# Moving the first expert block's row fetch, turn and split into the last attention heads, and the quarter blocks' table to the fifth block

## The chip, the cores and the metric

The kernel runs on one core of a Trainium2 chip. The metric is the device time of one execution in microseconds (us). The engines named below are TensorE (PE; its weight loads are PEld), VectorE (DVE), ScalarE (ACT), GpSimd (POOL) and the queue of SyncE (SP), from which nearly all DMAs are issued.

## The reference

Attention over 8 batches and 8 heads, sequence 576, head width 64, with a causal mask and a bias from a running sum; its output is taken as 4608 tokens of width 512. Each token then goes to one of 8 experts (argmax of a gate) and through that expert's two matrices, and is scaled by the gate's probability. Cut to what matters:

```python
def _attn_ref(q, k, v, s):
    scores = scale * np.matmul(q, k.transpose(0, 1, 3, 2))
    cum = np.cumsum(np.maximum(s, 0.0), axis=-1)
    bias = -(cum[:, :, :, None] - cum[:, :, None, :])
    scores = np.where(causal, -1e9, scores + np.minimum(bias, 0.0))
    attn = softmax(scores)
    return np.matmul(attn, v)

def _moe_ref(x, modality_id, w_gate, modality_bias, w1, w2):
    logits = x @ w_gate + modality_bias[modality_id]
    e_idx, gate_w = argmax(logits), softmax(logits)[e_idx]
    for e in range(E):                       # E = 8, D = 512, F = 1024
        h = np.maximum(x[e_idx == e] @ w1[e], 0.0)
        out[e_idx == e] = gate_w * (h @ w2[e])
```

## The kernel before

**Attention.** The 64 (batch, head) pairs are worked two at a time: a "pair" index runs from 0 to 31, eight pairs for each of four groups of batches. Every pair has nine score tiles, so the loop in Attn.run has 288 steps k and a few more to run out. A step makes one score tile (PE, then DVE for mask and maximum, then ACT for the exponential), turns the tile of three steps earlier (trans) and goes on with a tail: probabilities times V (L474), a copy of the result (ACT, L477, and DVE, L481), a matmul that turns it to rows and adds the gate's logits (L492, L494, by way of the helper at L346), and a DVE multiplication that writes it to the tile x of its group (L497, L499). The second tail of the last pair is the last work of attention.

**Routing.** When a group of batches is done, Route.group computes the experts of its tokens, counts with a small matmul (L708), and scatters the rows by nine indirect DMAs from POOL (L732) to a list for each expert in DRAM. It is a generator; attention's loop runs a piece of it at each step (the list bg). Groups 0 to 2 are scattered (27 scatters) during attention, group 3 afterwards. From the counts of groups 0 to 2 Route.first makes a table t2 of six full blocks of 256 rows. Moe.early then reads expert and row of block 0 to registers and, from step 278 (EARLY), loads its first four weight chunks and splits them on POOL into a high and a low part (L963, L966).

**Experts.** All matrix products are made in three passes over high and low parts. A block of 256 rows takes eight weight chunks of 512 KB: four of w1 (matmuls at L1102) and four of w2 (L1077). Chunks are loaded by SP, copied (high part) by ACT (L965) and subtracted (low part) by DVE (L966); their buffers come in three sets, wca, wcb and wcc. The rows of a block are fetched by gather2: four DMAs for 512 columns (L1038) and one for the gate and token number (L1039). Moe.xt turns them on DVE into PSUM (L1052), and splits them by an ACT copy (L1054) and a DVE subtraction (L1055). This is done in the middle of the block before; for block 0 it is done at the start, after attention's pools have closed. ACT and DVE empty the two halves of a block's output (L1087, L1085), and POOL scatters it to the result (L1088).

**Order.** The program is ordered by a scheduler that takes, on each engine, the ready instruction of best priority; a with-block of high_priority moves its instructions forward by so many places, and issue_after puts instructions behind a given one on its engine, without a wait between engines. Block 0 is traced with an offset of 300 (PRI), group 3's routing with 900 (PRI2).

**Remaining tables.** Block 2 is preceded by Route.rest, some 65 small DVE instructions: the table t3 (12 full blocks) and then the table t4 of the quarter blocks (64 rows), which are worked at the very end. The call for each block is finish(k); in blocks 1 to 4 it also writes zero rows behind the lists (pad).

Of the kernel before, what the change touches and what calls it, by code (L numbers as in the profile page):

```python
# [7 lines left out]
F32 = mybir.dt.float32  # L8
F32R = mybir.dt.float32r
BF16 = mybir.dt.bfloat16  # L10
I32 = mybir.dt.int32
AF = mybir.ActivationFunctionType
ALU = mybir.AluOpType
# [4 lines left out]
P = 128  # L18
KW = 576
XW = 72  # L20
# [18 lines left out]
class Attn:  # L39
# [415 lines left out]
    def tail(self, st, g):  # L455

        nc = self.nc
        V, PT, x, h = st["V"], st["PT"], st["x"], st["h"]
# [4 lines left out]
        oT = self.oT  # L463
# [12 lines left out]
        self.wall = m.ins  # L476
        nc.scalar.copy(oT[:, q0:q0 + 256], o[:, :256])  # L477
        if g:
            for ab in range(2):
                r = slice(64 * ab, 64 * ab + 64)  # L480
                nc.vector.tensor_copy(oT[r, 512 + 64 * ab:576 + 64 * ab], o[r, 256:320])  # L481
        yield
# [13 lines left out]
        rv = rs[:, 4 * g:4 * g + 4].unsqueeze(2).broadcast_to([P, 4, XW])  # L496
        nc.vector.tensor_tensor(x[g][:, :, :, h], src.rearrange("p t (d r) -> p t d r", r=2), rv.rearrange("p t (d r) -> p t d r", r=2), ALU.mult)  # L497
        if g:
            nc.vector.tensor_scalar(x[2][:, 0, :, h], xo[:, 4 * XW:5 * XW].rearrange("p (d r) -> p d r", r=2), rs[:, 8:9], None, ALU.mult)  # L499

# [75 lines left out]
PRI = 300  # L576
PRI2 = 900
SCS = 5, 5, 4, 4
NRA, NRB = 2, 4
# [4 lines left out]
NGS = 0  # L584
EARLY = 278


class Route:
# [81 lines left out]
    def group(self, bp, x, psum, mm, then=None):  # L670
# [34 lines left out]

        of = ohb.rearrange("p t e -> p (t e)")
        for u in range(10):
            (mm or nc.tensor.matmul)(pp[:, 8 * u:80], self.tri[:, min(u, 1)], of[:, :80 - 8 * u], start=u == 0, stop=u == 9)  # L708
# [142 lines left out]
    def rest(self):  # L851
# [25 lines left out]
        nc.vector.scalar_tensor_tensor(base, ex, float(CAP), s, ALU.mult, ALU.add)  # L877
        self.t3 = self.rows("r", nb, 2, ex, base, cn)

        exh, bh, ch = ex[:, N3:], base[:, N3:], cn[:, N3:]  # L880
# [25 lines left out]
class Moe:  # L906
    def __init__(self, ctx, tc, R, w1, w2, ident, out):
        self.nc, self.tc, self.R, self.w1, self.w2, self.ident, self.out = tc.nc, tc, R, w1, w2, ident, out
        self.wa = ctx.enter_context(tc.tile_pool(name="mwa", bufs=1))
        self.wb = None  # L910
        self.n = 0
        self.last = [None] * 4
        self.hold = None
        self.late, self.stop = None, 1 << 30
        self.back = ()

    def open(self, ctx):
# [114 lines left out]
    def gather2(self, tb, b, r):  # L1032

        nc = self.nc
        xr = self.mx.tile([P, 8, P], F32, name="xr", bufs=2)
        tg = self.mx.tile([P, 2, 2], F32, name="tg", bufs=3)
        rows = self.R.lists[bass.ds(r, 2 * P), :]
        i = [nc.sync.dma_start(xr[32 * q:32 * q + 32], rows[:, P * q:P * q + P].rearrange("(t p) d -> p t d", p=32)).ins for q in range(4)]  # L1038
        i.append(nc.sync.dma_start(tg, rows[:, 512:514].rearrange("(u p) d -> p u d", u=2)).ins)  # L1039
        self.rows(tb, i)  # L1040
        oi = self.mp.tile([P, 2], I32, name="oi", bufs=3)
        nc.vector.tensor_tensor(oi, tg[:, :, 1], tb["past"][:, bass.ds(b, 1), :].rearrange("p b u -> p (b u)"), ALU.add)
        return (xr, tg), oi

# [212 lines left out]
    def early(self):  # L1257
# [5 lines left out]
        for j in range(self.NA):  # L1263
# [4 lines left out]
            yield False  # L1268

    def run(self, lst, early=False, then=None, routed=None):  # L1270

        def pre(k):
            tb, b, nu = getattr(self.R, lst[k][0]), lst[k][1], lst[k][2]
            if nu == 0:
                e, r = zip(*(self.regs(tb, b + q) for q in range(2)))
                self.stop = self.n + 14
            else:
                e, r = self.er if early and k == 0 else self.regs(tb, b)
            xg, oi = self.gather(tb, b, r, nu)
            x = self.xt(xg, nu) if k == 0 else None  # L1280
            W, self.more = self.weights(e, self.have if early and k == 0 else ()) if nu else self.weights2(e)
            for _ in range(0 if self.late is not None else 2 if k else 8):
                next(self.more, 0)
            return W, xg, oi, x
# [27 lines left out]
def build(tc, qkv, s, mid, wg, mb, w1, w2, out):  # L1312
    nc = tc.nc
    with ExitStack() as ctx:
# [9 lines left out]
        with ExitStack() as actx:  # L1324
# [18 lines left out]

            setup = {**A.more, 5: A.consts, 14: R.consts, 17: lambda: A.save(0), 26: lambda: A.save(1), 20: lambda: R.setup(mid, mb, A.t1p)}
            bg = A.run(32, newx, done, setup)
            assert len(bg) == 1
            for _ in range(NGS):
                next(bg[0][0])
        with ExitStack() as mctx:
# [3 lines left out]
            def routed():  # L1353
                with ExitStack() as after:
                    for i in M.tr:
                        after.enter_context(tc.issue_after(i.ins))
                    after.enter_context(tc.high_priority(offset=PRI2))
                    for _ in bg[0][0]:
                        pass
                xctx.close()  # L1360
                M.open2(mctx)

            def finish(k):
# [3 lines left out]
                if 1 <= k <= 4:  # L1367
                    with ExitStack() as after:
# [3 lines left out]
                        if k == 2:  # L1372
                            for _ in R.rest():
                                pass
# [35 lines left out]
```

## Time and profile before

| what | value |
|---|---|
| median of 3 runs | 818.26 us (817.53 to 819.53) |
| the profiled execution's own time | 818.24 us |
| its span, first to last instruction | 816.5 us |
| mean granted TensorE clock | 0.992 |
| PE busy | 796.9 us, 98% |
| DVE busy | 575.3 us, 70% |
| ACT busy | 529.7 us, 65% |
| POOL busy | 364.4 us, 45% |

Starts in the profile are in us from the first instruction. A timeline row gives start, length, engine, line, operation, output and inputs, shape and count, and in brackets how long the engine was idle before and what released it. Attention's last matmul ends at 376.3 us; the experts fill the rest. The granted clock is the share of full clock that TensorE was given; it is 1.00 in most windows.

### The profile page before, as it was taken

Reading aid. Unit: us, or ns where it says so; the run is one execution under the profiler, and the core shown is the slowest. Engines: PE = TensorE matmul, PEld = TensorE weight load, DVE = VectorE, ACT = ScalarE, POOL = GpSimd, SP = SyncE. Lnnn points to the kernel's source line nnn. Section 1 sums busy time; section 2 is a strip of 40 time slices with the busy share of each in tenths; the row PEclk is TensorE's granted clock in tenths of the full one; section 3 lists DMA queues with packets and bytes.
Section 4 is the critical chain, followed back from the end, with each engine's and each line's share of the span. In section 5 each row is a group of like instructions: output and inputs, shape, how many; then the busy total and the mean of one; then the engine's idle time right before and its main releaser. Section 6 shows DMA issues by size and latency. Waiting matters only on the chain. (4 is left out here: it accounts for less than half of the span.)

```text
span 816.5 us, 16747 instructions
## 1 busy us (share of the span) xinstructions
PE 796.9 (98%) x5548; PEld 681.4 (83%) x5548; DVE 575.3 (70%) x1441; ACT 529.7 (65%) x1196; POOL 364.4 (45%) x383
## 2 busy tenths in 40 slices
PE   7999999999999999998999799999999999999997
PEld 6777887888888888877888798889899989988884
DVE  7666667667666677767679677777877766777654
ACT  6888788888878888875463355555555554455553
POOL 8959778988699877993600111100000010000001
PEclk9999999999999999999999999999999999999999
DMA  7665556776557666738696968677887878786750
GB/s 237 178 197 184 181 184 198 228 240 191 173 183 224 200 184 183 238 130 277 205 366 235 313 224 270 223 248 241 266 259 225 263 253 268 243 269 222 249 194 29
DMA packets 88134, 181.17 MB, mean 222 GB/s; under 512 B 13753, under 2 KB 33081, under 8 KB 87918
## 3 DMA queue, kind: packets, MB, share of 16 engines
q1 hardware_dynamic: 82206, 160.03, 62.2%
q0 software_dynamic: 5840, 20.06, 6.3%
q8 instruction: 44, 0.72, 0.4%
q14 instruction: 44, 0.36, 0.1%
HBM read 143.59 MB, written 26.80 MB: 209 GB/s over the span
## 5 line engine op out<-in xcount | busy, mean ns | idle before, releaser
L1088 POOL DMA_INDIRECT out<-ys,oi x36 | 39.0, 1084 | 357.1 <-ACT ys L1087 264.8
L396 DVE CUSTOM_DVE_ANT_0 pe<-sp,mk 128x512 f32<-128x512 f32 (+3 forms) x256 | 122.4, 488 | 100.6 <-PE sp L394 90.5
L416 ACT ACTIVATE pe<-pe,mx 128x512 f32<-128x512 f32 (+3 forms) x256 | 144.9, 567 | 15.7 <-DVE mx L396 13.1
L433 PE MATMUL pt<-ident,pe 128*128 128x128 f32 x640 | 110.7, 278 | 0.8 <-ACT PT L437 0.5
L437 ACT COPY PT<-pt 128x512 f32<-128x512 f32 (+1 forms) x192 | 97.3, 510 | 20.1 <-PE pt L433 20.1
L372 PE MATMUL sp<-KA,QH 128*128 128x256 f32 (+2 forms) x256 | 102.4, 402 | 2.5 <-POOL KA L236 2.5
L1104 ACT ACTIVATE hT<-hp 128x512 fp32r<-128x512 f32 x72 | 43.2, 600 | 89.5 <-PE hp L1102 87.7
L474 PE MATMUL o<-PT,V 128*64 128x320 f32 (+4 forms) x896 | 100.7, 364 | 0.0
L474 PEld LDWEIGHTS o<-PT,V 128*64 128x64 f32 x896 | 58.6, 136 | 46.6 <-issue 14.5
L1102 PE MATMUL hp<-xT,wcb 128*128 128x256 f32 x648 | 90.6, 283 | 0.8 <-DVE hT L1105 0.6
L1102 PE MATMUL hp<-xT,wca 128*128 128x256 f32 x624 | 87.1, 284 | 2.6 <-ACT xT L1054 2.5
L326 POOL TENSOR_TENSOR KA<-rawk,KA 64x576 fp32r<-64x576 f32 x62 | 87.2, 1425 | 0.2
L433 PEld LDWEIGHTS pt<-ident,pe 128*128 128x128 f32 x640 | 75.9, 143 | 13.6 <-issue 5.3
L326 POOL TENSOR_TENSOR QL<-rawq,QH 64x576 fp32r<-64x576 f32 x62 | 86.7, 1413 | 0.2
L394 PE MATMUL sp<-KB,QL 76*128 76x256 f32 (+2 forms) x256 | 85.4, 337 | 0.0
L1102 PEld LDWEIGHTS hp<-xT,wcb 128*128 128x128 f32 x648 | 83.4, 188 | 1.9 <-DVE hT L1105 0.8
L1102 PEld LDWEIGHTS hp<-xT,wca 128*128 128x128 f32 x624 | 80.3, 193 | 3.6 <-issue 2.6
L1105 DVE SCALAR_TENSOR_TENSOR hT<-hp,hT 128x512 fp32r<-128x512 f32 x72 | 49.5, 688 | 47.2 <-ACT hT L1104 46.9
L1077 PE MATMUL y<-wcb,hT 128*128 128x512 f32 x336 | 80.7, 396 | 0.0
L1077 PEld LDWEIGHTS y<-wcb,hT 128*128 128x128 f32 x336 | 62.7, 188 | 14.6
L1102 PE MATMUL hp<-xT,wcc 128*128 128x256 f32 x456 | 65.3, 282 | 4.8 <-DVE xT L1055 2.9
L1102 PEld LDWEIGHTS hp<-xT,wcc 128*128 128x128 f32 x456 | 59.3, 191 | 6.3 <-DVE xT L1055 3.1
(284 smaller groups left out, 1603.1 us busy)
## 6 DMA issues: line engine op xcount, KB each, us to landing
wrbw<-in_w SPq DMA_DIRECT2D x104, 512.0 KB
wraw<-in_w SPq DMA_DIRECT2D x56, 512.0 KB
rawq<-in_qkv SPq DMA_DIRECT2D x31, 576.0 KB
rawk<-in_qkv SPq DMA_DIRECT2D x31, 576.0 KB
V<-in_qkv SPq DMA_DIRECT2D x32, 320.0 KB
xr<-lists SPq DMA_DIRECT2D x72, 128.0 KB
KB<-KA SPq DMA_DIRECT2D x62, 144.0 KB
lists<-z SPq DMA_DIRECT2D x8, 576.0 KB
```

Of the source, the lines that this page charges most:

```text
L326: self.last = nc.gpsimd.tensor_tensor(o, i, h, ALU.subtract).ins
L372: self.pe.append(self.nc.tensor.matmul(sp[:, :nn], QH[:, q0:q0 + P], self.KA[u][:, ab, :nn], start=True, stop=False).ins)
L394: self.pe.append(nc.tensor.matmul(sp[:, :nn], QL[:EXT, q0:q0 + P], KB[:EXT, ab, :nn], start=False, stop=True).ins)
L396: ins = nc.vector.tensor_tensor_reduce(out=t[:, :n], in0=sp[:, :n], in1=self.mk[:, 512 - n:512], scale=-0.125, scalar=3.0e38, op0=ALU.add, ...
L416: self.act = nc.scalar.activation(t[:, :n], t[:, :n], AF.Exp, bias=m, scale=-1.0, accum_out=st["sums"][:, o:o + 1]).ins
L433: self.pe.append(nc.tensor.transpose(out=pt[:, o:o + P], in_=pe[:, P * j:P * j + P], identity=self.ident).ins)
L437: cp(w[:, :, :, v:v + P], pt[:, :n * (1 + both)].rearrange("p (a j q) -> p a j q", a=1 + both, q=P))
L474: m = nc.tensor.matmul(o[r, f - q0:q1 - q0], V[:, ab, j, :], PT[:, ab, PTS * j + f if j < 4 else PTW - 64:PTS * j + q1 if j < 4 else PTW], ...
L1077: self.last[0] = nc.tensor.matmul(y[u], hT[:, a, f, P * u:P * u + P], W[4 + f // 2][:, c, 512 * (f % 2):512 * (f % 2) + 512], start=f == 0 ...
L1102: nc.tensor.matmul(hp[:, u], W[k][:, a, f:f + P], xT[:, c, k], start=k == 0 and i == 0, stop=k == 3 and i == 2)
L1104: hi = nc.scalar.activation(hs, hp, AF.Relu)
L1105: lo = nc.vector.scalar_tensor_tensor(hT[:, 1, 2 * m:2 * m + 2], hp, 0.0, hs.bitcast(F32), ALU.max, ALU.subtract)
```

## The change

- **Block 0's rows.** A new generator, Moe.early_rows, joins bg at step 275. When 27 scatters are issued and block 0's registers are known, it takes the two x tiles of group 2, which are scattered by then, as memory, and issues the five DMAs of the rows. It goes on at step 288 (TURN), after the last score tile: two DVE transposes, now from SBUF into SBUF, each followed by a copy on POOL (high part); at steps 289 and 290 one DVE subtraction each (low part), put behind the newest of the DVE steps called behind_x. Block 0 uses these tiles and no PSUM for them. The splits of w2's four chunks of block 0 are put behind attention's last ACT copy and last DVE multiplication (fin) instead of behind block 0's row split.
- **Group 3's routing.** The part up to the counting matmul keeps the offset 900; from that matmul on, with the scatters, it has 200 (PRI3).
- **Tables.** Route.rest stops after t3 in block 2; t4 is made when finish(4) is called.

```diff
@@ Attn.tail
-        nc.scalar.copy(oT[:, q0:q0 + 256], o[:, :256])
+        self.fin = [nc.scalar.copy(oT[:, q0:q0 + 256], o[:, :256])]
...
-                nc.vector.tensor_copy(oT[r, 512 + 64 * ab:576 + 64 * ab], o[r, 256:320])
+                self.behind_x = nc.vector.tensor_copy(oT[r, 512 + 64 * ab:576 + 64 * ab], o[r, 256:320])
...
-        nc.vector.tensor_tensor(x[g][:, :, :, h], ...)
+        self.fin.append(nc.vector.tensor_tensor(x[g][:, :, :, h], ...))
         if g:
-            nc.vector.tensor_scalar(x[2][:, 0, :, h], ...)
+            self.behind_x = nc.vector.tensor_scalar(x[2][:, 0, :, h], ...)
@@ Route.group
         of = ohb.rearrange("p t e -> p (t e)")
+        if not mm:
+            yield "mm"
@@ Route.rest
         self.t3 = self.rows("r", nb, 2, ex, base, cn)
+        yield "t3"
@@ Moe
+    def early_rows(self, pool, A):
+        nc, R = self.nc, self.R
+        while len(R.scat) < 27 or self.er is None:
+            yield False
+        a, b = (pool.tile([P, 4, XW // 2, 8, 2], F32, name="x").rearrange("p t d h r -> p (t d h r)") for _ in range(2))
+        tg, oi = R.c.tile([P, 2, 2], F32, name="tg0"), R.c.tile([P, 2], I32, name="oi0")
+        xr, xf = a[:, :1024].rearrange("p (t d) -> p t d", t=8), a[:, 1024:2048].rearrange("p (k n) -> p k n", k=4)
+        xT = b[:, :2048].bitcast(F32R).rearrange("p (a k n) -> p a k n", a=2, k=4)
+        self.fetch_rows(R.t2, self.er[1], xr, tg)
+        yield TURN
+        ks = [slice(0, 2), slice(2, 4)]
+        for k in ks:
+            A.hold[0] = nc.vector.transpose(out=xf[:, k].rearrange("p k (t n) -> p k t n", n=32),
+                                            in_=xr.rearrange("p t (d k) -> p k t d", k=4)[:, k]).ins
+            A.last = nc.gpsimd.tensor_scalar(xT[:, 0, k], xf[:, k], 1.0, 1.0, ALU.mult, ALU.mult).ins
+        for k in ks:
+            yield False
+            with self.tc.issue_after(A.behind_x.ins):
+                nc.vector.tensor_tensor(xT[:, 1, k], xf[:, k], xT[:, 0, k].bitcast(F32), ALU.subtract)
+        nc.vector.tensor_tensor(oi, tg[:, :, 1], R.t2["past"][:, 0], ALU.add)
+        self.first = ((None, tg), oi), xT
@@ Moe.run, pre(k)
-            xg, oi = self.gather(tb, b, r, nu)
-            x = self.xt(xg, nu) if k == 0 else None
+            if early and k == 0:
+                (xg, oi), x = self.first
+            else:
+                xg, oi = self.gather(tb, b, r, nu)
+                x = self.xt(xg, nu) if k == 0 else None
@@ build
+            setup[275] = lambda: M.early_rows(xps[0], A)
             bg = A.run(32, newx, done, setup)
+            M.tr = None, *A.fin
...
-                    for i in M.tr:
+                    for i in M.tr[1:]:
                         after.enter_context(tc.issue_after(i.ins))
-                    after.enter_context(tc.high_priority(offset=PRI2))
-                    for _ in bg[0][0]:
-                        pass
+                    with tc.high_priority(offset=PRI2):
+                        while next(bg[0][0]) != "mm":
+                            pass
+                    with tc.high_priority(offset=PRI3):
+                        for _ in bg[0][0]:
+                            pass
...
                         if k == 2:
-                            for _ in R.rest():
+                            rest.append(R.rest())
+                            while next(rest[0]) != "t3":
+                                pass
+                        if k == 4:
+                            for _ in rest[0]:
                                 pass
```

More of the change, by code (lines that the diff above doesn't have):

```diff
@@ L496, in tail @@
         rv = rs[:, 4 * g:4 * g + 4].unsqueeze(2).broadcast_to([P, 4, XW])
-        nc.vector.tensor_tensor(x[g][:, :, :, h], src.rearrange("p t (d r) -> p t d r", r=2), rv.rearrange("p t (d r) -> p t d r", r=2), ALU.mult)
+        self.fin.append(nc.vector.tensor_tensor(x[g][:, :, :, h], src.rearrange("p t (d r) -> p t d r", r=2), rv.rearrange("p t (d r) -> p t d r", r=2), ALU.mult))
         if g:
-            nc.vector.tensor_scalar(x[2][:, 0, :, h], xo[:, 4 * XW:5 * XW].rearrange("p (d r) -> p d r", r=2), rs[:, 8:9], None, ALU.mult)
+            self.behind_x = nc.vector.tensor_scalar(x[2][:, 0, :, h], xo[:, 4 * XW:5 * XW].rearrange("p (d r) -> p d r", r=2), rs[:, 8:9], None, ALU.mult)
     def run(self, npair, newx, done, setup):
@@ L577 @@
 PRI2 = 900
+PRI3 = 200
 SCS = 5, 5, 4, 4
@@ L585 @@
 EARLY = 278
+TURN = 288
 class Route:
@@ L915, in __init__ @@
         self.back = ()
+        self.er = None
     def open(self, ctx):
@@ L1036, in gather2, with fetch_rows @@
         tg = self.mx.tile([P, 2, 2], F32, name="tg", bufs=3)
+        oi = self.mp.tile([P, 2], I32, name="oi", bufs=3)
+        self.fetch_rows(tb, r, xr, tg)
+        nc.vector.tensor_tensor(oi, tg[:, :, 1], tb["past"][:, bass.ds(b, 1), :].rearrange("p b u -> p (b u)"), ALU.add)
+        return (xr, tg), oi
+    def fetch_rows(self, tb, r, xr, tg):
+        nc = self.nc
         rows = self.R.lists[bass.ds(r, 2 * P), :]
@@ L1040, in gather2 @@
         self.rows(tb, i)
-        oi = self.mp.tile([P, 2], I32, name="oi", bufs=3)
-        nc.vector.tensor_tensor(oi, tg[:, :, 1], tb["past"][:, bass.ds(b, 1), :].rearrange("p b u -> p (b u)"), ALU.add)
-        return (xr, tg), oi
     def xt(self, xg, nu):
@@ L1354, in routed @@
                 with ExitStack() as after:
-                    for i in M.tr:
+                    for i in M.tr[1:]:
                         after.enter_context(tc.issue_after(i.ins))
-                    after.enter_context(tc.high_priority(offset=PRI2))
-                    for _ in bg[0][0]:
-                        pass
+                    with tc.high_priority(offset=PRI2):
[4 more added lines that the diff above has]
+                            pass
                 xctx.close()
                 M.open2(mctx)
+            rest = []
             def finish(k):
```

## The prediction

> **What bounds the kernel now.** I read the page first, for which engine the span belongs to, then the waits of TensorE, then the timeline around the two places where it waits, and last the granted clock there.
>
> ```profile
> PE 796.9 (98%) x5548; PEld 681.4 (83%) x5548; DVE 575.3 (70%) x1441; ACT 529.7 (65%) x1196; POOL 364.4 (45%) x383
> ```
>
> TensorE (PE) carries the span; only what shortens its idle time or its own work can pay. Its longest waits in the expert stage (waited for; total us, times, longest us) are two:
>
> ```profile
> PE hp L1102 <- ACT xT L1054: 3.3, 2, 2.5
> PE hp L1102 <- DVE xT L1055: 2.9, 1, 2.9
> ```
>
> The first is the step from attention to the experts. Timeline of PE:
>
> ```profile
> 375.56 0.76 PE L346 MATMUL ox<-pw,oT 128*128 128x144 f32 x4 [0.47 <-ACT oT L477]
> 378.77 8.47 PE L1102 MATMUL hp<-xT,wca 128*128 128x256 f32 x54 [2.45 <-ACT xT L1054]
> ...
> 387.37 5.20 PE L1102 MATMUL hp<-xT,wca 128*128 128x256 f32 x42
> 392.40 11.39 PE L1077 MATMUL y<-wcb,hT 128*128 128x512 f32 x48
> ```
>
> Attention's last matmul ends at 376.32, block 0's first starts at 378.77: 2.45 us idle. The same matmul then runs slow: 54 in 8.47 us, but 42 in 5.20, by which 54 take 6.69; 1.78 us are lost. The clock says why. Windows of 3.41 us: start and end, length, PE busy (instructions), granted clock, DMA share, GB/s.
>
> ```profile
> 377.19:380.60 3.41, 1.72 (x12) 1.00 1.11 320
> 380.60:384.01 3.41, 3.41 (x19) 0.50 1.13 293
> ...
> 448.87:452.28 3.41, 2.13 (x16) 1.00 0.90 280
> 452.28:455.69 3.41, 0.55 (x4) 1.00 1.02 374
> 455.69:459.10 3.41, 3.41 (x17) 0.50 1.09 241
> ```
>
> A window with 1.72 or 0.55 us of work is followed by one at half clock; one with 2.13 is not. Half clock for 3.41 us costs 1.71 us of matmul time each.
>
> The second place is the start of block 3. Timeline of PE, with block 5's start for comparison:
>
> ```profile
> 448.73 1.64 PE L1102 MATMUL hp<-xT,wca 128*128 128x256 f32 x12
> 451.20 0.39 PE L1102 MATMUL hp<-xT,wcc 128*128 128x256 f32 x1 [0.83 <-ACT xT L1054]
> 452.04 0.62 PE L1102 MATMUL hp<-xT,wcc 128*128 128x256 f32 x3 [0.45 <-DVE wcc L966]
> 455.51 1.09 PE L1102 MATMUL hp<-xT,wcc 128*128 128x256 f32 x4 [2.86 <-DVE xT L1055]
> ...
> 502.69 0.51 PE L1102 MATMUL hp<-xT,wcc 128*128 128x256 f32 x2 [0.64 <-DVE wcc L966]
> ```
>
> The gaps sum to 4.14 us. The length of a whole block is read from the ACT step that empties its first output:
>
> ```profile
> 448.24 0.69 ACT L1087 ACTIVATE ys<-y,tg 128x512 f32<-128x512 f32 x1 [0.94 <-PE y L1077]
> 477.03 0.69 ACT L1087 ACTIVATE ys<-y,tg 128x512 f32<-128x512 f32 x1 [2.71 <-PE y L1077]
> 499.75 0.69 ACT L1087 ACTIVATE ys<-y,tg 128x512 f32<-128x512 f32 x1 [4.45 <-PE y L1077]
> 523.70 0.69 ACT L1087 ACTIVATE ys<-y,tg 128x512 f32<-128x512 f32 x1 [1.99 <-PE y L1077]
> ```
>
> Block 3 takes 28.79 us, block 4 22.72, block 5 23.95. Block 3's excess over block 4 is 6.07, of which gaps and half clock explain 5.85. What VectorE (DVE) did instead of block 3's rows:
>
> ```profile
> 440.15 0.16 DVE L883 TENSOR_SCALAR hn<-rcn 128x7 f32<-128x7 f32 x1
> ...
> 442.47 0.36 DVE L777 TENSOR_TENSOR hoh<-hoh,ha 128x196 f32<-128x196 f32 x1
> ...
> 449.41 1.12 DVE L1052 STREAM_TRANSPOSE tp<-xr 128x512 f32<-128x512 f32 x1
> ...
> 454.77 0.68 DVE L1055 TENSOR_TENSOR xT<-tp,xT 128x512 fp32r<-128x512 f32 x1
> ...
> 455.38 0.17 DVE L809 TENSOR_SCALAR hpast<-hpast 128x28 f32<-128x28 f32 x1
> ```
>
> From the first to the last of these rows stand the 34 instructions of the quarter blocks' table. The first thirteen, to L777's end at 442.8, have DVE nearly to themselves for 2.6 us; the other twenty-one are strewn among weight splits and take 3.6 us from one start to the next: 6.2 us in all, 6.1 of them ahead of the split at 454.77 that PE waited for.
>
> **The change part by part.**
>
> *First block's rows.* After the last attention step two transposes, two ACT copies and two DVE splits go from the path. They now happen earlier, so the question is what makes them late. The rows involved, for DVE, POOL and the SP queue:
>
> ```profile
> 374.69 0.28 DVE L499 TENSOR_SCALAR xq<-ox,rs 128x72 f32<-128x72 f32 x1
> 376.72 1.08 DVE L1052 STREAM_TRANSPOSE tp<-xr 128x512 f32<-128x512 f32 x1
> ```
>
> ```profile
> 356.43 0.99 POOL L732 DMA_INDIRECT lists<-xq,di  x1 [0.17 <-issue]
> 365.50 1.05 POOL L963 TENSOR_SCALAR wca<-wraw 128x1024 fp32r<-128x1024 f32 x1 [1.31 <-DMA wraw<-in_w]
> 370.10 2.36 POOL L966 TENSOR_TENSOR wca<-wraw,wca 128x1024 fp32r<-128x1024 f32 x1
> ```
>
> ```profile
> 361.89 2.69 SPq L940 DMA_DIRECT2D wraw<-in_w  x2
> ...
> 369.32 1.89 SPq L1038 DMA_DIRECT2D xr<-lists  x4
> 371.40 0.41 SPq L1039 DMA_DIRECT2D tg<-lists  x1
> ```
>
> ```profile
> 359.00:360.00 1.00, 1.00 0.00 0
> ```
>
> The fetch is five DMAs, 1.89 + 0.41 = 2.30 us of the SP queue. It must wait for the 27th scatter (POOL, 356.43). No byte moves between 359 and 360 (that window's DMA share is 0.00), so the scatter has landed by 359 and the fetch is issued by about 361.7, ahead of the third weight load at 361.89. Queued behind it on SP are that load, the fourth, and the last V; the first feeds POOL. I let the 0.5 MB of rows delay that weight load by 0.8 us (bounds 0 and 2.3, the whole issue time). POOL's last weight split then ends at 373.3 instead of 372.46. Its two new copies of 128x512 follow, 0.53 each by half of the 1.05 row (upper bound 1.05): done at 374.3. The transposes, into SBUF now, are priced as the row into PSUM, 1.08 (bounds 0.5 and 2.2), on a DVE that between its last score step and 374.69 waits for attention's tail. The second split is put behind L499, so from 374.97 by 0.68: 375.7. That is before 376.32, when PE comes free, so the 2.45 us go, and with 377.19 to 380.60 busy the half clock too: 2.45 + 1.78 = 4.23. Bounds: 4.70, if PE also fills the 0.47 gap, and 0, if the rows are as late as now. If the cover fails (fetch delays the weights by 2.3), the split ends near 376.6 and 0.3 is lost.
>
> *Next late thing.* Block 0's second half needs the w2 chunks, at 392.40 before, about 388.2 then. Their splits hang on attention's last ACT and DVE steps instead of on the row splits, so they start earlier too; I cost this at nothing.
>
> *Group 3's positions and scatter at a lower priority.* Same instructions, somewhat later; block 6 is the first to use them. Costed at nothing (see the last rival).
>
> *Table moved from block 2's to block 4's DVE queue.* Windows of both blocks: length, PE, PEld, DVE, ACT, POOL busy, clock, DMA.
>
> ```profile
> 425.00:449.00 24.00, 24.00 (x153) 21.60 (x152) 22.59 (x72) 11.05 (x15) 2.02 (x2) 1.00 0.74 258
> ...
> 477.00:500.00 23.00, 23.00 (x146) 20.76 (x146) 14.96 (x17) 11.12 (x15) 2.96 (x2) 1.00 0.87 298
> ```
>
> In block 2 DVE is busy 22.59 of 24 us and owes the next block its rows. Taking 6.1 us out puts the late split at 448.7 instead of 454.77, ended at 449.4; PE's first twelve matmuls last from 448.73 to 450.37. So the long gap closes. I leave block 3 the excess that block 5 shows without any table, 23.95 - 22.72 = 1.23: gain 6.07 - 1.23 = 4.84 (bounds 0 and 6.07). Block 4 gets the 6.2 us: 14.96 + 6.2 = 21.2 of 23, so it fits, but the small instructions go in front of weight splits that PE wants within a microsecond: bounds 0 and 6.07 (what the two tables together cost behind block 2), taken 0.5, two or three small ones, near the end with room. The quarter blocks come last, far from needing the table.
>
> Sum against the profiled execution's own 818.24 (the runs' median is 818.26): 818.24 - 4.23 - 4.84 + 0.5 = 809.7.
>
> **The rivals.**
>
> *The table's stall only moves.* Block 5 takes block 3's excess: 4.84 come back, 814.5. For it: block 5 already starts with 0.64 us short. Against: 8.0 us of DVE idle in block 4, against 1.4 in block 2.
>
> *The rows come no earlier than attention's end.* POOL's copies slip behind something, or the fetch waits: 818.24 - 4.84 + 0.5 = 813.9. It needs xT at 378.77, three microseconds later than worked out.
>
> *The half clock is not the gaps' doing.* If it comes with the start of dense expert matmuls, gaps close and both slow windows stay: 809.7 + 2 x 1.71 = 813.1. Against: 448.87 to 452.28 with 2.13 us busy is followed by full clock, and both slow windows follow emptier ones. The Trainium skill, TensorE: Matmul & The Clock Gate, "What's actually happening", has the array fall to half rate after at least one idle window of about 3.4 us. Taken word for word that would not be met by a gap of 2.45 us, and would speak for this rival and 813.1; the trace has the fall after a window half busy, and my sum goes by the trace.
>
> *Slower: group 3's scatter is held too long.* By the order in which the pools open, the third weight set (wcc) lies over the memory of group 3's rows, so it can't be written before they are scattered.
>
> ```profile
> 390.06 1.07 POOL L732 DMA_INDIRECT lists<-x,di  x1 [2.22 <-DMA wraw<-in_w]
> ```
>
> ```profile
> 414.72 1.05 ACT L965 CAST wcc<-wrbw 128x1024 fp32r<-128x1024 f32 x1 [1.87 <-DMA wrbw<-in_w]
> ```
>
> ```profile
> 417.71 8.56 PE L1077 MATMUL y<-wcc,hT 128*128 128x512 f32 x36
> ```
>
> With everything 4.2 us earlier the first copy is due at 410.5. Four scatters and their landing take some 8 us, so a start after 402 begins to cost, and one after about 412 eats the 9 us gained; at 415, 25 us later than now, 821. Nothing in the priorities suggests so much.
>
> **How the numbers follow.** Forecast 0.64 (own range 807.5 to 812); stall moved 0.11; rows late 0.12; half clock stays 0.05; both gains lost or undone 0.04; slower 0.04. The likeliest gives 809.7. The range goes from 806.8 (0.47 and most of block 3's and 5's excess gained) to 814.5, which takes in the first three rivals. 0.3%, 2.5 us, is about what can be told from no change: faster 0.90, within 0.06, slower 0.04.
>
> **What would show it.** Right: no wait above 0.5 us between L346's last and L1102's first matmul; y of block 0 near 388; no 0.50 clock in either place; block 3 under 24 us; L883 to L809 in block 4, and blocks 4 and 5 together not over 47.2 us. Wrong: a wait of PE for POOL's copies or for weights at the seam, block 5 near 28 us, or a copy to the third weight set that waits for a scatter.

## The result and the profile after

The changed kernel takes 822.99 us (median of 4, 822.06 to 824.13), the kernel before 818.26: a ratio of 1.0055 (95% interval 1.0041 to 1.0069). It is 4.7 us slower where 8.5 us less were forecast. The profiled execution took 822.06 us, its span is 820.3.

The page of the changed kernel, engines, and its longest waits of PE in the expert stage (us in all, times, longest):

```profile
PE 798.8 (97%) x5548; PEld 682.5 (83%) x5548; DVE 576.2 (70%) x1441; ACT 526.7 (64%) x1194; POOL 364.9 (44%) x385
```

```profile
PE hp L1113 <- DVE hT L1116: 4.4, 3, 3.0
PE y L1088 <- ACT wcc L971: 2.3, 1, 2.3
```

The work is the same, and the two waits for row splits that led the list before are gone. Two others stand in their place: matmuls that wait for the hidden layer's split (hT) and a second half that waits for weights. In the new file L1102, L1077, L1087, L1104, L1105, L1054 and L1055 are L1113, L1088, L1098, L1115, L1116, L1065 and L1066; the weight copy and split L965 and L966 are L971 and L972, the row turn L1052 is L1063.

The lengths of the blocks come from the same ACT step as in the prediction, timeline of ACT in the changed kernel:

```profile
400.30 0.69 ACT L1098 ACTIVATE ys<-y,tg 128x512 f32<-128x512 f32 x1 [2.80 <-PE y L1088]
427.60 0.69 ACT L1098 ACTIVATE ys<-y,tg 128x512 f32<-128x512 f32 x1 [4.49 <-PE y L1088]
450.15 0.69 ACT L1098 ACTIVATE ys<-y,tg 128x512 f32<-128x512 f32 x1 [1.95 <-PE y L1088]
473.90 0.69 ACT L1098 ACTIVATE ys<-y,tg 128x512 f32<-128x512 f32 x1 [4.82 <-PE y L1088]
504.00 0.69 ACT L1098 ACTIVATE ys<-y,tg 128x512 f32<-128x512 f32 x1 [2.60 <-PE y L1088]
526.92 0.69 ACT L1098 ACTIVATE ys<-y,tg 128x512 f32<-128x512 f32 x1 [1.79 <-PE y L1088]
```

| us | before | after | difference | forecast |
|---|---|---|---|---|
| block 0's output begins | 403.13 | 400.30 | -2.83 | -4.23 |
| block 1 | 22.48 | 27.30 | +4.82 | 0 |
| block 2 | 22.63 | 22.55 | -0.08 | 0 |
| block 3 | 28.79 | 23.75 | -5.04 | -4.84 |
| block 4 | 22.72 | 30.10 | +7.38 | +0.5 |
| block 5 | 23.95 | 22.92 | -1.03 | 0 |

The sum is +3.2; the spans differ by 3.8. So both stalls that were to go did go, and two new ones, in blocks 1 and 4, cost more.

**The place where attention ends.** Timelines after, of POOL's row copies, DVE's second row split and PE:

```profile
373.22 1.20 POOL L1296 TENSOR_SCALAR x<-x 128x512 fp32r<-128x512 f32 x2
```

```profile
375.55 0.68 DVE L1300 TENSOR_TENSOR x<-x 128x512 fp32r<-128x512 f32 x1
```

```profile
375.78 0.73 PE L346 MATMUL ox<-pw,oT 128*128 128x144 f32 x4 [0.59 <-DVE xq L499]
376.25 5.91 PE L1113 MATMUL hp<-x,wca 128*128 128x256 f32 x48
382.01 0.21 PE L712 MATMUL rt<-ohb,tri 128*128 128x80 bf16 x1
382.87 2.39 PE L1113 MATMUL hp<-x,wca 128*128 128x256 f32 x18 [0.65 <-DVE hT L1116]
```

The expert matmul follows attention's last one without a bracket, at 376.25 instead of 378.77, and 48 of them take 5.91 us, 0.123 each, against 0.124 in the 42 that took 5.20 before; no window from there to 415 has half clock.

**Block 1.** Timelines of PE, of DVE and of ACT:

```profile
417.27 0.74 PE L1088 MATMUL y<-wcc,hT 128*128 128x512 f32 x2 [2.26 <-ACT wcc L971]
418.54 9.72 PE L1088 MATMUL y<-wcc,hT 128*128 128x512 f32 x34 [0.53 <-DVE wcc L972]
```

```profile
412.93 0.69 DVE L1116 SCALAR_TENSOR_TENSOR hT<-hp,hT 128x512 fp32r<-128x512 f32 x1 [2.10 <-ACT hT L1115]
413.54 1.08 DVE L1063 STREAM_TRANSPOSE tp<-xr 128x512 f32<-128x512 f32 x1
```

```profile
414.66 0.59 ACT L1065 CAST xT<-tp 128x512 fp32r<-128x512 f32 x1 [1.76 <-DMA wraw<-in_w]
415.69 0.59 ACT L1065 CAST xT<-tp 128x512 fp32r<-128x512 f32 x1 [0.45 <-DVE tp L1063]
416.17 2.00 ACT L971 CAST wcc<-wrbw 128x1024 fp32r<-128x1024 f32 x2
```

The weight copy at 416.17 has no bracket: it waits for nothing but the two row copies ahead of it on ACT. They wait for the turns of block 2's rows, and these stand behind the fourth split of block 1's hidden layer. (The bracket at 414.66 names a weight DMA, as the last thing that happened before the step; the turn itself ends only 0.04 us ahead of it, at 413.54 + 1.08 = 414.62, and in the kernel with early preparation below the same idle time of 1.76 is put down to the turn.) In the kernel before, the turns stood behind the first split, 5.7 us earlier, although block 0 ended later there:

```profile
407.28 0.69 DVE L1105 SCALAR_TENSOR_TENSOR hT<-hp,hT 128x512 fp32r<-128x512 f32 x1 [2.07 <-ACT hT L1104]
407.89 2.12 DVE L1052 STREAM_TRANSPOSE tp<-xr 128x512 f32<-128x512 f32 x2
```

**Block 4.** Timelines of PE, of DVE (the first and last of the 34 table rows, and between them the hidden split that PE waited for) and of ACT:

```profile
475.58 0.50 PE L1113 MATMUL hp<-xT,wcb 128*128 128x256 f32 x2 [0.29 <-ACT wcb L971]
476.84 0.98 PE L1113 MATMUL hp<-xT,wcb 128*128 128x256 f32 x6 [0.76 <-DVE wcb L972]
...
479.60 0.50 PE L1113 MATMUL hp<-xT,wca 128*128 128x256 f32 x2 [0.65 <-DVE wca L972]
...
487.07 2.08 PE L1113 MATMUL hp<-xT,wcb 128*128 128x256 f32 x9 [2.97 <-DVE hT L1116]
```

```profile
475.28 0.16 DVE L888 TENSOR_SCALAR hn<-rcn 128x7 f32<-128x7 f32 x1
...
486.33 0.68 DVE L1116 SCALAR_TENSOR_TENSOR hT<-hp,hT 128x512 fp32r<-128x512 f32 x1
...
490.70 0.18 DVE L813 TENSOR_SCALAR hpast<-hpast 128x28 f32<-128x28 f32 x1
```

```profile
481.61 0.60 ACT L1115 ACTIVATE hT<-hp 128x512 fp32r<-128x512 f32 x1 [2.29 <-PE hp L1113]
```

ACT had done its part of the hidden layer at 482.2; DVE came to its own at 486.33, since table rows and weight splits stood ahead of it. The granted clock of both places (columns as in the prediction):

```profile
415.70:419.11 3.41, 1.31 (x5) 1.00 0.81 329
419.11:422.53 3.42, 3.42 (x10) 0.51 0.79 241
483.94:487.35 3.41, 0.44 (x3) 1.00 0.98 213
487.35:490.76 3.41, 3.41 (x18) 0.50 0.98 352
```

Behind the gaps of each place comes a window at half clock besides, 1.7 us of matmul time. Block 1: 2.26 + 0.53 + 1.7 = 4.5 of its 4.82. Block 4: 0.29 + 0.76 + 0.16 + 0.65 + 2.97 + 1.7 = 6.5 of its 7.38 (the 0.16 is a split of the same line at 477.98).

### The profile page after: what moved, and what is told of

It reads as the page before. It is cut to its first block, busy times and chain, and to the rows that moved or that the text cites. A ratio compares the mean times of both kernels' runs of the same rounds, so it can differ in the third digit from the quotient of the medians.

```text
span 820.3 us, 16744 instructions
## 1 busy us (share of the span) xinstructions
PE 798.8 (97%) x5548; PEld 682.5 (83%) x5548; DVE 576.2 (70%) x1441; ACT 526.7 (64%) x1194; POOL 364.9 (44%) x385
## 5 line engine op out<-in xcount | busy, mean ns | idle before, releaser
L1115 ACT ACTIVATE hT<-hp 128x512 fp32r<-128x512 f32 x72 | 43.1, 599 | 93.4 <-PE hp L1113 93.1
L1113 PE MATMUL hp<-xT,wcb 128*128 128x256 f32 x648 | 91.8, 285 | 4.2 <-DVE hT L1116 3.0
L1113 PEld LDWEIGHTS hp<-xT,wcb 128*128 128x128 f32 x648 | 84.7, 191 | 6.0 <-DVE hT L1116 3.4
L1116 DVE SCALAR_TENSOR_TENSOR hT<-hp,hT 128x512 fp32r<-128x512 f32 x72 | 49.6, 688 | 49.1 <-ACT hT L1115 48.9
L1088 PE MATMUL y<-wcb,hT 128*128 128x512 f32 x336 | 80.8, 396 | 0.0
L1088 PEld LDWEIGHTS y<-wcb,hT 128*128 128x128 f32 x336 | 62.6, 188 | 14.6
L1113 PE MATMUL hp<-xT,wca 128*128 128x256 f32 x528 | 73.7, 280 | 0.6 <-DVE wca L972 0.6
L1113 PEld LDWEIGHTS hp<-xT,wca 128*128 128x128 f32 x528 | 67.3, 189 | 1.4 <-DVE wca L972 0.8
L1088 PE MATMUL y<-wcc,hT 128*128 128x512 f32 x264 | 65.0, 402 | 2.8 <-ACT wcc L971 2.3
L1113 PE MATMUL hp<-xT,wcc 128*128 128x256 f32 x456 | 65.1, 281 | 1.5 <-DVE wcc L972 0.8
```

What stands on the lines that cost most here:

```text
L1088: self.last[0] = nc.tensor.matmul(y[u], hT[:, a, f, P * u:P * u + P], W[4 + f // 2][:, c, 512 * (f % 2):512 * (f % 2) + 512], start=f == 0 ...
L1113: nc.tensor.matmul(hp[:, u], W[k][:, a, f:f + P], xT[:, c, k], start=k == 0 and i == 0, stop=k == 3 and i == 2)
L1115: hi = nc.scalar.activation(hs, hp, AF.Relu)
L1116: lo = nc.vector.scalar_tensor_tensor(hT[:, 1, 2 * m:2 * m + 2], hp, 0.0, hs.bitcast(F32), ALU.max, ALU.subtract)
```

## The experiments

Each kernel is told by its difference from the changed one, where no other is named. Ratios are to the kernel before on the same chip, with 95% intervals. Executions of one kernel differ by 1.4 to 7.3 us, so block lengths of the profiled one and medians are read together. The ACT step by which blocks are measured sometimes starts about 1 us late, after PE has gone on to the next block; where that matters, the length is given by PE's last matmul of each block instead.

**The rows alone** (both tables in block 2 again):

```diff
-    rest.append(R.rest())
-    while next(rest[0]) != "t3":
-        pass
-if k == 4:
-    for _ in rest[0]:
+    for _ in R.rest():
         pass
```

> The rows part alone: the quarter blocks' table is made again in block 2, the rest is the changed kernel. My theory now is that the four places are separate: seam -2.8 us, block 1 +4.8, block 3 back to about 28.8 us and block 4 to about 22.7. Sum against the kernel before: +2.0, so about 820.3 us (819 to 821.5). Rival, that block 1's loss came from the table's place or from the whole schedule shifting: block 1 near 22.5 us again and a time near 815.5.

822.22 us, 1.0041 (1.0028 to 1.0054). Block 1 takes 27.30, block 3 30.69, block 4 22.71. The rows' half of the change is what makes block 1 long, and by itself makes the kernel slower: 2.9 us gained at attention's end (400.20), 4.8 lost in block 1 and 1.9 in block 3. The last wasn't expected: in block 3 two windows in a row have half clock (0.50 from 456.39 to 463.21), where the kernel before had one.

**The table alone** (the kernel before, with t4 made when finish(4) is called):

```diff
 if k == 2:
-    for _ in R.rest():
+    rest.append(R.rest())
+    while next(rest[0]) != "t3":
         pass
...
+if k == 4:
+    for _ in rest[0]:
+        pass
```

> The table part alone: the kernel before, with the quarter blocks' table made in block 4. My theory: block 3 shrinks by about 5 us to near 23.8, block 4 grows by about 7.4 to near 30, block 5 loses about 1: +1.3 against before, about 819.6 us (818 to 821). Rival, that block 4 stalls only because the rows part had shifted the weights: block 4 below 24 us and a time near 813.

816.64 us, 0.9985 (0.9971 to 0.9999). Block 3 falls from 28.79 to 23.26, block 4 rises from 22.72 to 26.63. With the 34 instructions in it block 4 is 3.9 us longer, less than the 7.4 with the rows moved too, which were expected here as well. PE waits four times there: 1.01, 0.16 and 0.52 for weight splits and 1.34 for the hidden split. How much of this is the table's is told by the kernel with the table in block 7, below.

**Zero rows one block later** (finish writes zero rows in blocks 2 to 5 instead of 1 to 4, so block 1 begins without them):

```diff
-if 1 <= k <= 4:
-    R.pad((2 * k - 2, 2 * k - 1))
+if 2 <= k <= 5:
+    R.pad((2 * k - 4, 2 * k - 3))
```

> The changed kernel with the zero rows behind the lists written in blocks 2 to 5 instead of 1 to 4. Theory: in block 1 the weight loads stand on the SP queue behind the two zero writes, and these wait for DVE after block 0's end; with that gone the first load of the third weight set is issued some 4 us earlier or more, the PE wait of 2.26 + 0.53 us and the slow window of block 1 vanish: block 1 near 22.6 us, total about 818.2 us. Rival, that the load is late because the DMA engines are full of group 3's rows and the load takes 6 us whenever issued, or that ACT's order holds the copy: block 1 stays above 26 us and the total within 1 us of 823.

817.36 us, 0.9988 (0.9977 to 0.9999). Timeline of DVE and ACT:

```profile
409.28 1.09 DVE L1063 STREAM_TRANSPOSE tp<-xr 128x512 f32<-128x512 f32 x1
```

```profile
411.94 2.00 ACT L971 CAST wcc<-wrbw 128x1024 fp32r<-128x1024 f32 x2
```

The turns stand behind the second hidden split (408.67), the weight copy starts 4.2 us earlier, PE waits for nothing between 400 and 425, and block 1 takes 22.41. That is its whole 4.8 us back, with all of the early rows kept; the median falls by 5.6 us against the changed kernel, though the two were not run side by side.

**The zero rows' preparation ahead** (the two small DVE steps that SP's zero writes wait for, and so the weight loads queued behind them, come early):

```diff
 with tc.high_priority(offset=PRI3):
     for _ in bg[0][0]:
         pass
+    R.pad(())
```

> The changed kernel, but the zero tile and the integer list ends are made on DVE right after group 3's positions, not after block 0's output; the zero writes stay in block 1. Theory: the SP queue in block 1 waits for these two DVE steps, which stand behind block 0's output and a weight split; with them early the first load of the third weight set is issued 3 us or more sooner and block 1 takes 22.5 to 23.5 us, total about 818.5 us. Rival, that the two writes of 576 KB themselves hold the loads back on the queue and the DMA engines: block 1 stays above 25.5 us, total above 821.

822.08 us, 1.0036 (1.0023 to 1.0049). This was the test of the transfer: SP issues the two chunks at 398.85 instead of 408.36. Timelines of SP and PE:

```profile
398.85 0.52 SPq L948 DMA_DIRECT2D wrbw<-in_w  x2
```

```profile
417.03 0.73 PE L1088 MATMUL y<-wcc,hT 128*128 128x512 f32 x2 [2.26 <-ACT wcc L971]
418.29 3.07 PE L1088 MATMUL y<-wcc,hT 128*128 128x512 f32 x12 [0.53 <-DVE wcc L972]
```

Chunks issued 9.5 us earlier, and the same two waits to 10 ns. The theory that block 1 waits for its weights' transfer falls, and with it the 22.5 to 23.5 us that were expected. Block 1 is 24.65 us by the ACT step, but that step starts late in block 0; by PE's last matmuls (400.75 and 426.49) it is 25.74, against 27.29 in the changed kernel. The 1.55 us are about the price of the slow window, which doesn't follow the waits here. The wait is the same to 10 ns in five kernels (these two, the rows alone, the table in pieces and group 3 at the old offset), as the sum of steps in a fixed order would be.

**Row copies behind the weight copies** (ACT's copies of block 2's rows put behind the copy of the chunk that PE waits for; DVE's order is left):

```diff
+self.cast = {}
...
-nc.scalar.copy(w[:, 0], raw)
+self.cast[n] = nc.scalar.copy(w[:, 0], raw)
...
-nxts.append(self.xt(nxt[1], lst[k + 1][2]))
+with (self.tc.issue_after(self.cast[15].ins) if early and k == 1 else ExitStack()):
+    nxts.append(self.xt(nxt[1], lst[k + 1][2]))
```

> The changed kernel with one order laid down: on ACT the two copies of block 2's rows stand behind the copies of the first two chunks of the third weight set. With the zero writes early, the chunk had landed 13 us before its copy and PE still waited 2.26 us, so the theory is now that the order of instructions makes block 1's wait: four hidden splits, DVE's turns of block 2's rows, ACT's row copies, then the weight copy, a chain that starts only when PE ends the first half. With the row copies behind, block 1 takes 22.4 to 23.3 us instead of 27.3 and the total falls by 4 to 5 us to about 818. Rival, that the chunk's landing (411.9) is what counts: block 1 stays above 25 us.

820.41 us, 1.0023 (1.0005 to 1.0040). Timeline of PE:

```profile
417.19 8.19 PE L1089 MATMUL y<-wcc,hT 128*128 128x512 f32 x34 [1.38 <-DVE wcc L973]
```

The wait falls from 2.26 + 0.53 to 1.38 and no slow window follows; block 1 takes 24.08, 3.2 less, though not the 22.4 to 23.3 that were expected. About half of the wait and the slow window hung on ACT's order; what is left is named by the bracket, DVE's split of the chunk.

**Group 3 at the old offset:**

```diff
-PRI3 = 200
+PRI3 = 900
```

> The changed kernel with group 3's second part at the old priority offset of 900. The ten counting matmuls stand together behind 27 matmuls of block 0 instead of strewn among them. Theory: strewing and the wait of 0.65 us for the hidden layer's split cost most of the 1.4 us that the seam gave less than forecast: block 0's output copy starts at about 399.3 instead of 400.3, block 1 and block 4 as in the changed kernel, total about 822. Rival, that the wait comes from the weight splits in front on DVE: output copy at 400.3 or later and no difference in the total.

821.78 us, 1.0034 (1.0017 to 1.0052). Block 0's output begins at 399.92, only 0.4 earlier, but the ACT step is late: PE's last matmul of block 0 ends at 399.79, against 400.97. From the first expert matmul (375.97, against 376.25) that is 23.82 us instead of 24.72, so the counting matmuls together save 0.9. Block 1 takes 26.99 by PE, with the same waits of 2.26 and 0.53. The lower priority is no cause of them.

**The table in pieces** (t4 cut into nine pieces, one in each block from 3 on, each put behind two given earlier instructions):

```diff
+yield "p"
...
-if k == 4:
-    for _ in rest[0]:
-        pass
+if 3 <= k <= 14:
+    with ExitStack() as after:
+        for i in (M.hold, M.last[1].ins):
+            after.enter_context(tc.issue_after(i))
+        next(rest[0], 0)
```

> The changed kernel with the quarter blocks' table made in ten pieces of two to seven small instructions, one piece in each block from block 3 on. Theory: block 4's 30.1 us come from 34 small DVE instructions in front of the weight splits and of the hidden layer's split; pieces of 0.6 us each fit: block 4 near 22.8, blocks 3 and 5 to 13 no longer than now by more than 0.3 each, total about 815.5 us (814.5 to 817). Rival, that block 4's weights come late by the SP queue or the DMAs: block 4 stays above 27 us and the total near 822.

819.08 us, 1.0007 (0.9996 to 1.0017). Block 4 falls from 30.10 to 25.06, block 5 rises from 22.92 to 26.31; block 1 stays at 27.14. The expected 814.5 to 817 is missed: blocks 4 and 5 hold only two and one of the small instructions, and are still 2.3 and 2.4 us longer than in the kernel before.

**Both** (zero rows later and the table in pieces):

> Zero rows written in blocks 2 to 5 and the table in ten pieces, together. If the two losses are separate they add: block 1 near 22.4 us, block 4 near 25 or below, block 5 at most 26.3; total 812 to 815 us, below the kernel before by 4 to 6. Rival, that a stall taken away only moves to the next block whose weights are split late: the sum of blocks 1 to 6 stays above 145 us and the total near 818.

816.76 us, 0.9974 (0.9959 to 0.9989), not the 812 to 815 that were expected. The profiled execution is the slowest of the twelve (821.57), with attention's end 4.6 us later than in the changed kernel. Block 1 takes 22.41 by PE, block 3 22.37, block 4 24.19, but blocks 5 and 6 25.06 and 25.32.

**The table in block 7** (zero rows later, t4 when finish(7) is called), and the same on the kernel before, without the early rows:

```diff
-if 2 <= k <= 5:
+if 2 <= k <= 5 or k == 7:
...
-if k == 4:
+if k == 7:
     for _ in rest[0]:
```

> Zero rows in blocks 2 to 5 and the whole table in one go, in block 7. Theory: 34 small DVE instructions ahead of weight splits cost most in a block whose first four chunks are still to be split when it starts; block 4 without the table is 23 to 25 us, and block 7, whose chunks are further ahead, loses 1 to 4 us over 22.57; total 812.5 to 816. Rival, that the price of the table is its DVE time and the same wherever it stands: block 7 near 30 us, total near 818.

> The kernel before with only the quarter blocks' table moved, to block 7. Theory: the place decides the table's price; block 3 falls to about 23.3 us as with the table in block 4, block 4 stays below 24 instead of 26.6, block 7 stays at 22.6: total about 814 us, better than the table in block 4 (816.6) and about as good as with the rows moved as well. Rival, that the rows part is worth its 2.8 us at the seam: this one is at least 2 us slower than the kernel with rows, zero rows and table moved (815.4).

With the early rows 815.41 us, 0.9955 (0.9938 to 0.9971); without them 816.80, 0.9977 (0.9964 to 0.9990). The two intervals overlap, so what the early rows add to the moved table isn't told apart from nothing. Block 7 takes 22.57 and 22.79, against 22.56 before: the 34 instructions lengthen it by at most 0.2. But block 4 doesn't become short without them. In the kernel before with the table in block 7 it takes 24.72, where below 24 was expected, and block 5 25.09. Timeline of PE at its block 4's start:

```profile
475.35 0.98 PE L1103 MATMUL hp<-xT,wcb 128*128 128x256 f32 x6 [1.01 <-DVE wcb L967]
```

The wait of 1.01 for a weight split that stood there with the table stands there without it too. So of the 3.9 us of block 4 with the table alone, 2.0 come with no table in it, and 1.9 with the table (its waits of 0.52 and 1.34). What the place of the table is worth has to be summed over blocks. From block 1's output to block 7's it takes 141.05 us with the table in block 4 and 140.58 with it in block 7 (medians 816.64 and 816.80); with early rows and late zero rows 143.77 and 141.94 (817.36 and 815.41). That is 0.5 and 1.8 us; the rest of what block 4 loses by the table comes back in the blocks behind it when it is gone.

**The last V ahead of the rows** (in the version with the table in block 7, where a matmul waited 0.27 us for V: V's DMA is issued at step 275; then also with the old offset):

```diff
-if k % 9 == 2 and pi > 1:
+if k % 9 == 2 and 1 < pi < npair - 1:
...
-setup[275] = lambda: M.early_rows(xps[0], A)
+def rows0():
+    A.V[31] = A.load_v(31)
+    return M.early_rows(xps[0], A)
+setup[275] = rows0
```

> The kernel with the zero rows in blocks 2 to 5 and the table in block 7, and the last pair's V issued on the SP queue at step 275, ahead of all but the first DMA of the rows. Theory: V, queued behind five row DMAs and two weight loads, lands between 369.4 and 373.3 in different executions and PE wants it at about 370.5, so some executions lose up to 2 us and a slow window; with V early this wait is gone and the median falls by 0.3 to 1.5 us, from 815.4 to about 814.5. Rival: V is rarely late and the median stays within 0.3 us.

> The same as the kernel with V early, and group 3's second part at offset 900, so that its ten counting matmuls stand together. Block 0's output came 0.4 us earlier with it; block 1 keeps 22 to 23 us if the order of rows and weight copies holds. Total within 1 us of the one with V early, rather below it.

818.64 us, 1.0002 (0.9985 to 1.0018), and 817.50, 0.9982 (0.9972 to 0.9993): slower than without, against the expectation. Timeline of POOL and PE in the first:

```profile
370.95 1.05 POOL L969 TENSOR_SCALAR wca<-wraw 128x1024 fp32r<-128x1024 f32 x1 [3.40 <-DMA wraw<-in_w]
...
375.55 2.36 POOL L972 TENSOR_TENSOR wca<-wraw,wca 128x1024 fp32r<-128x1024 f32 x1
```

```profile
378.35 0.44 PE L346 MATMUL ox<-pq,oT 128*128 128x72 f32 x2 [1.03 <-DVE oT L481]
...
380.43 0.73 PE L346 MATMUL ox<-pw,oT 128*128 128x144 f32 x4 [0.84 <-DVE xq L499]
```

With V and the rows ahead of the third weight load, POOL waits 3.40 us for it, 2.23 without V in front. Its last split and the row copies behind it come 1.2 us later by that, and attention's own last steps wait for DVE. The other profile, an execution nearer to its median (818.14), has the same two waits (1.1 and 0.8). The wait of 0.27 for V is gone and others of 1.03 and 0.84 have come. What more the median lost isn't explained; in the first profile (821.32, 2.7 above the median) the 27th scatter already comes 3.5 us later than in the version without V in front (359.80 against 356.26), ahead of anything that the edit moves.

**The small addition moved** (L1301, the scatter's row numbers, behind the second row split; in the V version, in the version with the table in block 7, and there with the old offset too):

```diff
-nc.vector.tensor_tensor(xT[:, 1, k], ...)
+lo = nc.vector.tensor_tensor(xT[:, 1, k], ...)
-nc.vector.tensor_tensor(oi, tg[:, :, 1], R.t2["past"][:, 0], ALU.add)
+with self.tc.issue_after(lo.ins):
+    nc.vector.tensor_tensor(oi, tg[:, :, 1], R.t2["past"][:, 0], ALU.add)
```

> The kernel with the last V issued ahead of three of the row DMAs, with one change: the small DVE addition that makes the scatter's row numbers (L1301, two inputs in SBUF, 0.15 us when nothing disturbs it) stands behind the second row split instead of ahead of attention's last copy. Theory 1 (the addition is held until POOL's running weight split ends, 1.85 us before, and attention's last copy L481 and multiplication L499 stand behind it): the PE waits of 1.03 for DVE's copy and 0.84 for xq shrink below 0.5 together, and the median falls from 818.64 to 816.8 to 817.5. Theory 2 (attention itself is longer, the addition only fills a time in which DVE had nothing to do): waits and median as they were, 818.3 to 819.

> The version with zero rows a block later and the table in block 7, with the same small addition moved. In the profile of that version it took 0.67 us and ended 0.16 us ahead of what the copy behind it waited for anyway. Theory 1 says the addition costs nothing in such an execution and up to a microsecond in those in which V and the weights land later: median 814.8 to 815.4 against 815.41. Theory 2: no difference, 815.2 to 815.7.

> The same with group 3's counting matmuls and scatters at the old offset of 900, which put the ten matmuls together and brought block 0's output 0.4 us earlier in the changed kernel: 0.4 less than the one without, 814.4 to 815.2. If the order of the blocks behind it changes with it, block 1 or 2 takes the gain back: 815.5 to 817.

817.38 us, 0.9987 (0.9974 to 1.0000); 815.94, 0.9964 (0.9953 to 0.9976); 813.82 (813.38 to 815.87), 0.9950 (0.9934 to 0.9965). In the V version the median fell by the 1.3 us that the first theory said (its interval overlaps that of the version without the move), but its waits did not shrink: the 1.03 is gone and the 0.84 has become 2.26, because DVE's first row split, ordered ahead of L497 and L499, waits for POOL's copies.

```profile
376.67 1.08 DVE L1300 TENSOR_TENSOR x<-x 128x512 fp32r<-128x512 f32 x1 [1.66 <-POOL x L1296]
```

```profile
378.57 0.73 PE L346 MATMUL ox<-pw,oT 128*128 128x144 f32 x4 [2.26 <-DVE xq L499]
```

So that the addition held attention's end up isn't shown: the move changed the order of the splits too. In the table's version it changes nothing (815.94 against 815.41). The third kernel has the lowest median, 4.9 us below the 818.72 of the kernel before in the same runs (4.1 by the ratio), but its interval overlaps those of the second and of the table in block 7 alone. Timeline of PE in it:

```profile
379.21 0.41 PE L712 MATMUL rt<-ohb,tri 128*128 128x80 bf16 x10 [0.45 <-DVE ohb L698]
```

The ten counting matmuls stand together. From the first expert matmul to block 0's output it takes 398.48 - 375.32 = 23.16 us, against 24.05 in the changed kernel (400.30 - 376.25) and in the second version (399.98 - 375.93); the forecast had been 0.4. The profiles of the last two differ by 1.4 us: these 0.9, and 0.6 by which attention ends earlier (375.32 against 375.93), which the edit doesn't touch. The rest of the 2.1 between their medians isn't located.

## Why the prediction was wrong

**The two gains were right in kind.** At attention's end the idle 2.45 us and the half clock went, as worked out: the rows were issued early, POOL's copies ended at 374.4 (forecast 374.3) and the second split at 376.2 (forecast 375.7), just in time for PE at 376.25. The gain at block 0's output is 2.83, not 4.23, because 0.65 for a hidden split and the strewn counting matmuls came behind it. Putting the latter together gave 0.9 of the missing 1.4 in both versions that tried it, in spite of a new wait of 0.45 for their input. Block 3 lost 5.04, forecast 4.84.

**The step that failed first is "Next late thing", costed at nothing.** It looked at the chunks of block 0's second half. The late thing was in block 1: row turns of block 2, now behind four hidden splits instead of one, ahead of a weight copy whose slack in the kernel before was 417.71 - 414.72 - 1.05 = 1.9 us, less than the 5.7 by which the turns moved. No duration of the old trace was mis-sized; the order of instructions that the scheduler lays down, which I took as given outside the edited lines, had changed. That it is the order and not the transfer is shown by the chunks issued 9.5 us earlier (wait unchanged), by the reordered ACT (half of the wait gone) and by the zero rows moved (all 4.8 us gone). Why the scheduler orders the turns so late with the rows early isn't shown. The runs show only that the turns come two hidden splits earlier when block 1 writes no zero rows; with the zero rows' preparation early they stay late.

**The second is the size of the table in block 4**: 0.5 taken from bounds of 0 and 6.07, measured 7.38, outside. Blocks 4 and 5 together take 53.0 us, where the prediction allowed 47.2. The reasoning was by room: 21.2 of 23 us of DVE. Room in the block is not room where the splits are wanted. Seven weight splits and a hidden split lie between 475.28 and 487.01, and with them 17 of the 34 small rows, the last of which ends at 490.88. The row on which 0.5 rested (block 5's small waits) came from a block with no table at all. But not all of the 7.38 is the table's. The first three waits of block 4 (0.29, 0.76, 0.16) stand ahead of most of its rows, and come at block 5's start as 0.31, 0.76 and 0.16 when the table is in block 7. Summed over blocks 2 to 7, having the table in block 4 instead of block 7 costs 1.8 us with the rows early and 0.5 without. So the block's length was mis-sized by 6.9 us, and part of that is a stall that would have come a block later.

**The first rival was partly right.** The stall does move. In the fastest version blocks 2 to 6 take 23.59, 22.37, 23.88, 25.05 and 24.62 us, 119.5 in all, against 120.2 before: block 3's 6.4 us are nearly all given back in the others. The same is seen without the early rows: with the table in block 7, blocks 4 and 5 grow by 2.0 and 1.1 us with no table in them. The sign of how is in ACT's and PE's timelines of the fastest version:

```profile
490.69 0.69 ACT L1098 ACTIVATE ys<-y,tg 128x512 f32<-128x512 f32 x1 [4.83 <-PE y L1088]
491.27 1.04 ACT L971 CAST wcc<-wrbw 128x1024 fp32r<-128x1024 f32 x1
```

```profile
492.36 0.50 PE L1113 MATMUL hp<-xT,wcc 128*128 128x256 f32 x2 [0.31 <-ACT wcc L971]
```

ACT idles 4.83 us in front of an output copy that needs PE's last matmul, with weight copies ordered behind it that wait for nothing else; so the next block begins short (0.31 here, and 0.76 for the split that follows). That this order is the cause is argued from the rows; what would come of copying ahead of that step was not tried.

**The other rivals.** The rows came early; the half clock goes with the gaps, since it went with them at 377 and 455 and came with new ones at 419 and 487. The slower rival named group 3's scatter; the sign was right, the place and cause were not, and its chance of 0.04 rested on one mechanism where any change of order counts.

## What to carry to other kernels

In a program ordered by a scheduler, an edit can change the order of instructions well beyond its own lines, here a whole block later; so list, for the stages behind the edit, which in-order engine holds a step that PE needs within two microseconds, and put a price on its being pushed back. An engine's idle time counts only where it lies: compare the moved work with the idle time ahead of each split that PE waits for, not with the block's sum. Judge a moved stall by the sum over several blocks, since what one block gains the next may give back. When a wait comes back to 10 ns in kernels whose transfers differ by microseconds, look for a fixed order before a DMA.

## What the runs showed of the hardware

**The same gaps came with and without a slow window.** Gaps of 2.26 and 0.53 us gave one in the changed kernel and none in the kernel with early preparation. Windows of the latter, on the 3.41 us grid on which its clock changes:

```profile
412.86:416.28 3.42, 1.91 (x9) 1.00 0.03 11
416.28:419.69 3.41, 2.14 (x8) 1.00 0.11 29
419.69:423.10 3.41, 3.41 (x17) 1.00 0.95 268
```

The gaps are split over two windows with 1.91 and 2.14 us of work, and both pass; in the changed kernel one window had 1.31 and the next fell to 0.51. But busy time alone draws no line. In the table in pieces, block 5's start has waits of 0.31, 0.76 and 0.15 us:

```profile
499.84:503.25 3.41, 2.18 (x14) 1.00 0.25 92
503.25:506.67 3.42, 3.42 (x17) 0.50 0.88 297
```

A window with 2.18 us of work is followed by half clock here (one with 2.19 in the first V version too), while 1.91, 2.13 and 2.14 were not; and with the table in block 7 the same three waits, to 10 ns, are followed by full clock (block 5 takes 25.03 us there, 26.31 here). So 1.7 us can come or go with the same waits, and what decides isn't shown; where they fall on the grid is the likely reason. The Trainium skill, TensorE: Matmul & The Clock Gate, "What's actually happening", asks for at least one idle window of about 3.4 us before the fall; the windows ahead of a fall were 13 to 64% busy, and the measurement decides.

**A small DVE step was held by a running POOL step.** The addition of 128x2 values, in the V version, in POOL's last split beside it, and in the fastest version with POOL idle:

```profile
376.07 1.85 DVE L1301 TENSOR_TENSOR oi<-tg,no 128x2 int32<-128x2 f32 x1
```

```profile
375.22 0.15 DVE L1302 TENSOR_TENSOR oi<-tg,no 128x2 int32<-128x2 f32 x1
```

It ends at 377.92, and POOL's split, quoted above, at 375.55 + 2.36 = 377.91. In the changed kernel it took 0.35 and ended at 373.28, POOL's split there at 373.27. The Trainium skill, SBUF — State Buffer, "SBUF: two separate sides", says that a DVE operation with two inputs in SBUF shares a port pair with GpSimd, and that the one that started holds it to its end; the rows agree. Whether these 1.7 us lengthened the kernel isn't shown: with the addition moved, PE's two waits there sum to 2.26 us instead of 1.87.
